# Own PSUM tiles for the first products of the experts, and a new table of priorities

## The chip, the cores and the metric

The kernel runs on one core of a Trainium2 chip. The metric is the device time of one execution in microseconds; for before it is the median of three runs. Engines are named as in the profile: PE is TensorE (matrix products), PEld its loading of weights, DVE VectorE, ACT ScalarE, POOL GpSimd, SP SyncE. A tile in PSUM holds results of products until another engine reads them; the widest accumulation here is [128, 512] fp32.

## The reference

Attention with 4 sink positions and a window of 128, then a layer of 8 experts of which each row takes two:

```python
# q, k, v: (4, 8, 768, 64)
scores = scale * np.matmul(q, k.transpose(0, 1, 3, 2))
keep = is_sink | in_window            # pos < 4, or 0 <= rel < 128
a = softmax(np.where(keep, scores, -1e9))
x = (a @ v).transpose(0, 2, 1, 3).reshape(3072, 512)

noisy = x @ w_gate + np.log1p(np.exp(x @ w_noise)) * noise   # 3072 x 8
top2, top2_w = the two largest of a row, softmax over the two
for e in range(8):                    # w1[e]: 512 x 1024, w2[e]: 1024 x 512
    for k in range(2):
        mask = top2[:, k] == e
        h = np.maximum(x[mask] @ w1[e], 0.0)
        out[mask] += top2_w[mask, k, None] * (h @ w2[e])
```

## The kernel before

**Two plans.** Every operation is given to a list scheduler (`Plan`) with an engine, an estimated length, a priority (a due time; the lowest goes first) and the keys that it reads and writes. `Plan.run` plays the operations through in model time, engine by engine, and then issues them in the order that comes out. So each engine's order is fixed in the program, and only semaphores between engines decide the times on the chip. `phase_one` holds attention, the logits, the routing of batches 0 to 2 and the first four row tiles of expert 0 (`FIRST`, gathered for the rows that batches 1 and 2 gave it, the fourth tile from batch 2 alone). `phase_two` holds the routing of batch 3 at priority -200 and then all experts, whose due times are worked out from 0 on (`when`, `step`).

The priorities of the attention stage come from the table `PR`: one number for each kind of step (score products `qk`, sink copies `pcopy`, transposes `ptr_c`, ...), with `_0` and `_9` for the first and last of a batch. Others set places: `gap` and `gap_8`, how many steps of attention lie between two pieces of a routing; `et`, from which step on the first row tiles come; `pc_pool`, how many of eight sink copies go to GpSimd; `stay`, how dear it is for TensorE to change the kind of product.

**An expert.** The rows of an expert are cut into pieces of three or four row tiles (for expert 0 four and then three, for the others three and then four). A piece q has eight groups f. For each group, TensorE makes twelve first products (`up`, L1048 to L1050: high part of the weights by high part of the rows, high by low, low by high, over four blocks of 128) into a PSUM tile H; ScalarE takes relu of it (`up_h`, L1097, the high part of h); VectorE takes what relu's rounding left (`up_l`, L1105, the low part of h, which reads H too). Then TensorE makes the second products of the group (`down`, L1116 to L1118, for the last tile L1121 and L1122) into four PSUM tiles Y that all groups of the piece add to. First products of the next group are due between them. In the last piece (`apart`) the first products of all eight groups come before its second products.

**PSUM.** A score tile S is [128, 2, 512] fp32, two accumulations wide, in a ring of two; it comes from a pool `wide` that lives through both phases. In phase two two more tiles of tag S are taken, and `plan.views` hands out their halves: H(k) is half k mod 2 of the one (`room`), X(i) half i mod 2 of the other (`pair`), which the routing and the row turns use. The first products of the first two groups (`AHEAD`) are issued by `up_ahead` at the end of phase one, into the same halves; from the third group on they are operations of phase two.

**Row tiles of expert 0.** `first_rows` gathers 128 rows by indirect DMA (L891), scales them on VectorE (L942), turns them on TensorE (`rows_turn`, L952; the fourth tile into a tile of tag S, the others into X), and splits them into a high part on ScalarE (L966) and a low part on VectorE (in the rows `sqn<-S,skn`, L215 being a helper that subtracts). They need the rank of a batch's rows (L714), the first product of its routing, and the places that come of it (L806). Logits are products L601 and transposes L609.

The loop that gives out the operations of the experts:

```python
if k >= AHEAD:
    op("PE", UP1 * width + .19, zu, lambda q=q, f=f: up(q, f), ..., w=[("H", k)], ...)
op("ACT", .06 + width / 1200, zu, lambda q=q, f=f: up_h(q, f), r=[("H", k)], w=[("hh", k)], u=[("h", k)])
op("DVE", .08 + width / 950, zu, lambda q=q, f=f: up_l(q, f), r=[("H", k), ("hh", k)], w=[("hl", k)], u=[("h", k)])
```

Of the kernel before, what the change touches and what calls it, by code (L numbers as in the profile page):

```python
# [9 lines left out]
F32 = mybir.dt.float32  # L10
# [10 lines left out]
PR = dict(cur=-8431.651, cur1=-7439.283, cur1_0=218.223, cur1_9=-1416.941, cur_0=0.0, cur_9=-191.213, dv=-2620.133,  # L21
          dv_0=-188.761, dv_9=-58.0, exps=-79.031, exps_0=-733.766, exps_9=-686.771, ga=0.0, gt=185.39, lg=-1781.795,
          load_qk=4173.715, load_v=245.644, mins=-994.502, mins_0=35.968, mins_9=5432.878, nosink=-4343.446,
          nosink_0=462.054, nosink_9=43.061, pcopy=-1854.216, pcopy_0=972.034, pcopy_9=77.513, plow=-3587.377,
          plow_0=-204.859, plow_9=-701.943, prev=-1305.7, prev_0=-151.842, prev_9=314.934, ptr=-349.555,
          ptr_0=-1749.435, ptr_9=-10.037, ptr_c=-3954.256, ptr_c_0=-264.44, ptr_c_9=56.179, ptr_m=-1635.596,
          ptr_m_0=182.224, ptr_m_9=-0.973, pv=-632.746, pv_0=479.582, pv_9=-76.04, pv_c=-4613.603, pv_c_0=-4.393,
          pv_c_9=16.777, qk=-1178.393, qk_0=631.58, qk_9=-3710.152, rows_c=12808.825, rows_c_0=-665.082,
          rows_c_9=-7472.954, rt=-15225.06, sink_c=-3756.417, sink_c_0=0.0, sink_c_9=16.368, sinks=-2.103,
          sinks_0=1336.99, sinks_9=-790.624, sub=-299.026, sub_0=1233.464, sub_9=50.854, sums=0.0, sums_0=723.554,  # L30
          sums_9=-13.305, sums_i=-3243.012, sums_i_0=-939.503, sums_i_9=-291.364, w1=4288.053, pctr_0=777.383,
          pctr=0.0, pctr_9=57.978, ga_l=-998.334, gt_l=111.981, ll=0.0, ua=22395.225, dv_pool=1, sm_act=10, cm_pool=9,
          pc_pool=0, gap_8=2, et=42, gap=1, stay=2496.59)
# [6 lines left out]
FIRST = 4  # L40
AHEAD = 2
# [7 lines left out]
class Plan:  # L49
# [5 lines left out]
    def __init__(self, nc, pools, rings, cold=0.0):  # L55
        self.nc = nc
        self.pools = pools
        self.rings = dict(rings)
        self.cold = cold
        self.live = {}  # L60
        self.views = {}
        self.shapes = {}
        self.count = {}
        self.ops = []
        self.touch = {}
        self.wrote = {}

    def get(self, tag, i, shape=None, dt=F32, pool="sb", pad=None):
        kx = (tag, i)
        if tag in self.views:  # L70
            x = self.views[tag](i)
            if shape is None:
                shape = self.shapes[kx]
            else:
                self.shapes[kx] = shape = (shape, pad)
            shape, pad = shape
            to = pad or shape
            x = x[:, :math.prod(to[1:])]
            if len(to) == 3:
                x = x.rearrange("p (a b) -> p a b", a=to[1])  # L80
            return x if to == shape else x[tuple(slice(0, n) for n in shape)]
# [163 lines left out]
def attention(tc, plan, cst, sh, kqs, v, vss, xbuf):  # L245
# [17 lines left out]

    def warm():
# [44 lines left out]
    def qk(n, a):  # L309
        g, j, _ = at(n, 2 * a)  # L310
        for h in range(2):
            r = slice(h * D, (h + 1) * D)
            p = get("S", 2 * n + a, [128, 2, 512], F32, "wide")[:, h, :2 * KW].rearrange("p (a b) -> p a b", a=2)
# [614 lines left out]
def rows_turn(plan, nc, cst, sh, e, t, size, ring, z):  # L928
# [15 lines left out]
    def spot():  # L944
        if ring == "S":
            return get(ring, ti, [128, 2, 512], F32, "wide")[:, 0, :].rearrange("p (c s) -> p c s", c=c)
        return get(ring, ti, [128, c, 128], F32, "ps")
# [91 lines left out]
def room(sh):  # L1039

    return sh.B * (sh.H // 2) * (sh.S // 128) + 1


# [20 lines left out]


def experts(tc, plan, cst, sh, w1, w2, xbuf, out):
# [97 lines left out]
    for q, (e, tiles, width) in enumerate(info):  # L1164
# [130 lines left out]
def phase_one(tc, nc, plan, ac, tail, cst, sh, kq, v, vs, w1, w2, xbuf, out):  # L1295
# [18 lines left out]
    def first_rows(t, ring, zg, zt):  # L1314
        gather(plan, nc, cst, sh, xbuf, 0, t, zg)
        weight(plan, nc, cst, sh, 0, t, zt)
        if ring == "S":
            plan.count["S"] = 2 * NJ * HP * sh.B - 1
# [136 lines left out]
```

## Time and profile before

| what | before |
|---|---|
| median of three runs | 787.09 us (786.73 to 788.6) |
| the profiled execution | 783.96 us |
| its span | 782.3 us, granted clock 0.998 |
| TensorE busy | 744.1 us, 95%, 4499 products |
| weight loads (beside the products) | 618.9 us, 79% |
| VectorE busy | 454.7 us, 58% |
| ScalarE busy | 333.4 us, 43% |
| GpSimd busy | 437.6 us, 56% |

The span is what the profiler saw of the engines' work in one execution; the time of that execution has a little more around it. Products overlap in the pipeline, so the duration of one in a timeline (0.34 us) is longer than the distance from its start to the next one's (0.17 us), and busy time counts the overlap once. In a timeline the bracket at the end of a row gives the engine's idle time just before it, and what ended that. The list of waits adds these up by the waiting line and the line that it waited for. Attention ends, and the experts begin, at about 186 us.

### The profile page before, as it was taken

What the parts mean: (1) busy time and instruction counts of PE and PEld (TensorE: products, weight loads), DVE (VectorE), ACT (ScalarE), POOL (GpSimd) and SP (SyncE); (2) the same over time, 40 slices, a digit from 0 to 9 for tenths busy, and PEclk for the clock granted to TensorE, in tenths of its full rate; (3) what the DMA queues carried; (4) which work ended last, traced back from release to release, by engine and by line L of the source; (5) the groups of instructions that cost most, each with busy time, mean ns of one, the idle gap of its engine ahead of it and who ended that gap; (6) DMA issues with size and microseconds to landing.
All of it is one profiled execution on the core that took longest, in us unless ns stands there. A gap on an engine that the chain in (4) does not pass through costs nothing.

```text
span 782.3 us, 12963 instructions
## 1 busy us (share of the span) xinstructions
PE 744.1 (95%) x4499; PEld 618.9 (79%) x4499; DVE 454.7 (58%) x1181; ACT 333.4 (43%) x927; POOL 437.6 (56%) x625
## 2 busy tenths in 40 slices
PE   9999998789999999999999999999999999999975
PEld 4667676566778898889888987898898889888864
DVE  7889998987754554645364446526544643464210
ACT  6987996784114413341333143323413431451211
POOL 7665878875246375356727462747275473747202
PEclk9999999999999999999999999999999999999999
DMA  6568698565636753553445363517452652544213
GB/s 221 175 169 203 203 261 216 138 162 132 168 96 127 238 110 50 156 138 57 94 127 131 53 134 114 109 40 155 123 101 47 172 134 36 125 133 71 26 16 41
DMA packets 58372, 97.80 MB, mean 125 GB/s; under 512 B 19232, under 2 KB 31776, under 8 KB 58304
## 3 DMA queue, kind: packets, MB, share of 16 engines
q1 hardware_dynamic: 44928, 69.34, 30.5%
q0 software_dynamic: 13376, 27.60, 20.3%
q8 instruction: 36, 0.59, 0.3%
q14 instruction: 32, 0.26, 0.1%
HBM read 68.51 MB, written 28.40 MB: 124 GB/s over the span
## 4 chain that ended last, share of the span: by engine, by line
PE 70%; DVE 9%; issue 7%; ACT 6%; POOL 3%; DMA 3%; POOLq 0%; SPq 0%; DVEq 0%; ACTq 0%
PE S L1048 11%; PE S L1050 10%; PE S L1049 10%; PE Y L1118 9%; PE Y L1116 9%; PE Y L1117 9%; PE S L315 2%; DMA xg<-x_rows,rt_idq 2%; PE X L406 2%; ACT cbuf L346 2%; PE P L380 1%; DVE h L1105 1%; PE X L409 1%; DVE xg L942 1%; POOL out L1140 1%
## 5 line engine op out<-in xcount | busy, mean ns | idle before, releaser
L897 POOL DMA_INDIRECT xg<-x_rows,rt_idq x174 | 176.1, 1012 | 62.2 <-issue 53.3
L1105 DVE SCALAR_TENSOR_TENSOR h<-S,h 128x384 fp32r<-128x384 f32 (+4 forms) x168 | 75.7, 470 | 203.5 <-ACT h L1097 153.2
L1097 ACT ACTIVATE h<-S 128x384 fp32r<-128x384 f32 (+4 forms) x128 | 64.3, 503 | 290.8 <-PE S L1050 210.1
L1048 PE MATMUL S<-skn,w 128*128 128x384 f32 (+4 forms) x512 | 177.7, 347 | 10.0 <-DVE h L1105 10.0
L1050 PE MATMUL S<-skn,w 128*128 128x384 f32 (+4 forms) x512 | 175.9, 344 | 0.0
L1049 PE MATMUL S<-sqn,w 128*128 128x384 f32 (+4 forms) x512 | 175.6, 343 | 0.0
L1140 POOL DMA_INDIRECT out<-y,idx x53 | 91.7, 1730 | 57.5 <-ACT y L1125 40.9
L1149 POOL COPY spacer<-h 1x1 f32<-1x1 f32 x88 | 28.7, 326 | 157.6 <-ACT h L1097 156.8
L1048 PEld LDWEIGHTS S<-skn,w 128*128 128x128 f32 x512 | 96.1, 188 | 22.4 <-DVE h L1105 10.4
L1049 PEld LDWEIGHTS S<-sqn,w 128*128 128x128 f32 x512 | 96.1, 188 | 6.2
L1050 PEld LDWEIGHTS S<-skn,w 128*128 128x128 f32 x512 | 96.0, 188 | 2.5
L1118 PE MATMUL Y<-w2a,h 128*128 128x512 f32 x192 | 76.1, 397 | 2.3 <-DVE h L1105 1.8
L1116 PE MATMUL Y<-w2a,h 128*128 128x512 f32 x192 | 75.7, 394 | 0.7 <-ACT h L1097 0.7
L1116 PE MATMUL Y<-w2b,h 128*128 128x512 f32 x192 | 76.1, 396 | 0.0
L1117 PE MATMUL Y<-w2b,h 128*128 128x512 f32 x192 | 75.8, 395 | 0.0
L1118 PE MATMUL Y<-w2b,h 128*128 128x512 f32 x192 | 75.8, 395 | 0.0
L1117 PE MATMUL Y<-w2a,h 128*128 128x512 f32 x192 | 75.6, 394 | 0.0
L315 PE MATMUL S<-kq 64*128 64x264 f32 (+1 forms) x384 | 56.4, 401 | 4.3 <-DVE cbuf L325 1.6
L215 POOL TENSOR_TENSOR cbuf<-cbuf,mn 128x528 f32<-128x528 f32 x48 | 51.4, 1076 | 13.4 <-DVE mn L335 5.5
L966 ACT ACTIVATE skn<-xtn 128x512 fp32r<-128x512 f32 (+2 forms) x46 | 27.9, 606 | 61.7 <-DVE xtn L957 54.7
L346 ACT ACTIVATE cbuf<-cbuf 128x132 f32<-128x132 f32 x160 | 48.0, 314 | 6.6 <-POOL cbuf L215 6.2
L1118 PEld LDWEIGHTS Y<-w2a,h 128*128 128x128 f32 x192 | 36.1, 188 | 14.0 <-DVE h L1105 4.8
(212 smaller groups left out, 1298.3 us busy)
## 6 DMA issues: line engine op xcount, KB each, us to landing
st<-in_w1l SPq DMA_DIRECT2D x32, 512.0 KB
st<-in_w2l SPq DMA_DIRECT2D x32, 512.0 KB
kq<-in_kq SPq DMA_DIRECT2D x15, 792.0 KB
out<-zt SPq DMA_DIRECT2D x31, 256.0 KB
vn<-in_v SPq DMA_DIRECT2D x16, 384.0 KB
x_rows<-xr SPq DMA_DIRECT2D x48, 128.0 KB
xg<-x_rows,rt_idq POOLq DMA_INDIRECT x174
st<-in_vs SPq DMA_DIRECT2D x4, 256.0 KB
```

The lines of the kernel that those rows point to most:

```text
L315: nc.tensor.matmul(p[:, :2 if j else 1], kq(g)[r, j // 2, 2 + j % 2, NS:], x[:, :2 if j else 1], start=True, stop=True)
L346: nc.scalar.activation(C(n)[:, u], C(n)[:, u], AF.Exp, scale=1.0 / math.sqrt(D), accum_out=get("sm", n, [128, 4])[:, u:u + 1])
L897: nc.gpsimd.indirect_dma_start(out=x[:, i, :], out_offset=None, in_=xbuf.rearrange("r (q d) -> (r q) d", d=sh.SW), in_offset=bass.Indirect ...
L1048: nc.tensor.matmul(p, w[:, 0], xh, start=(i == 0), stop=False)
L1049: nc.tensor.matmul(p, w[:, 0], xl, start=False, stop=False)
L1050: nc.tensor.matmul(p, w[:, 1], xh, start=False, stop=(i == sh.DM // 128 - 1))
L1097: nc.scalar.activation(get("h", FC * q + f, [128, 2 * 128 * FIRST], F32R)[:, :width], get("H", FC * q + f, [128, width], F32, "ps", [128, ...
L1105: nc.vector.scalar_tensor_tensor(h[:, o:o + s1 - s0], p[:, s0:s1], 0.0, h[:, s0:s1].bitcast(F32), op0=OP.max, op1=OP.subtract)
L1116: nc.tensor.matmul(p, hh, w[:, 0], start=(f == 0), stop=False)
L1117: nc.tensor.matmul(p, hh, w[:, 1], start=False, stop=False)
L1118: nc.tensor.matmul(p, hl, w[:, 0], start=False, stop=(f == FC - 1))
L1140: d = nc.gpsimd.indirect_dma_start(out=out, out_offset=bass.IndirectOffsetOnAxis(ap=c["idx"][:size(e, t), e, t:t + 1], axis=0), in_=get("y ...
```

## The change

**PSUM.** The pool `wide` and `plan.views` go. The score tiles S now belong to the PSUM pool of the attention phase (two of them are taken first, so that their place is set). Phase two has rings of its own in its own PSUM pool: two tiles H and two tiles X, each [128, 512] fp32. These take the place of tiles of phase one, and the pool of phase two makes the first user of such a tile wait for the last of the old one.

**No products at the end of phase one.** `up_ahead`, `AHEAD` and `room` go. The first products of the first two groups are operations of phase two like all others.

**Priority of expert 0's relu and low part.** For piece 0 these two steps get `zu - 400` instead of `zu`, ahead of the last routing's -200; the products keep `zu`.

**The table.** All numbers of `PR` are new, and `ua` is no longer used. Of the settings, `gap` goes from 1 to 2, `gap_8` from 2 to 3, `et` from 42 to 36, `pc_pool` from 0 to 2 and `stay` from 2496 to 1992.

```diff
-PR = dict(cur=-8431.651, cur1=-7439.283, cur1_0=218.223, cur1_9=-1416.941, cur_0=0.0, cur_9=-191.213, dv=-2620.133,
...
-          pc_pool=0, gap_8=2, et=42, gap=1, stay=2496.59)
+PR = dict(cur=-10653.273, cur1=-2090.412, cur1_0=-442.426, cur1_9=73.44, cur_0=-4.596, cur_9=0.0, dv=0.64,
...
+          gap_8=3, et=36, stay=1992.355)
-AHEAD = 2
...
-            p = get("S", 2 * n + a, [128, 2, 512], F32, "wide")[:, h, :2 * KW].rearrange("p (a b) -> p a b", a=2)
+            p = get("S", 2 * n + a, [128, 2, 512], F32, "ps")[:, h, :2 * KW].rearrange("p (a b) -> p a b", a=2)
...
-def up_ahead(plan, nc, cst, sh, f, z):
-
-    width = 128 * FIRST
-
-    def go(i):
-        up_block(plan, nc, sh, plan.get("S", room(sh), [128, 2, 512], F32, "wide")[:, f % 2, :width], 0, f, i, halves(plan, sh, 0), width)
-
-    for i in range(sh.DM // 128):
-        plan.op("PE", 3 * (width / 2400 + .016), z, lambda i=i: go(i),
-                r=[(x, 0, t) for x in ("xh", "xl") for t in range(FIRST)] + [w_tile(plan, 1, 0, f // 2)[0]], w=[("H", f)],
-                u=[("S", room(sh))])
...
-            if k >= AHEAD:
-                op("PE", UP1 * width + .19, zu, lambda q=q, f=f: up(q, f),
-                   r=[(x, e, t) for x in ("xh", "xl") for t in tiles] + [w_tile(plan, 1, e, f // 2)[0]], w=[("H", k)],
-                   u=[(nm, NP + q) for nm in ("skn", "sqn")])
-            op("ACT", .06 + width / 1200, zu, lambda q=q, f=f: up_h(q, f), r=[("H", k)], w=[("hh", k)], u=[("h", k)])
-            op("DVE", .08 + width / 950, zu, lambda q=q, f=f: up_l(q, f), r=[("H", k), ("hh", k)], w=[("hl", k)], u=[("h", k)])
+            op("PE", UP1 * width + .19, zu, lambda q=q, f=f: up(q, f),
+               r=[(x, e, t) for x in ("xh", "xl") for t in tiles] + [w_tile(plan, 1, e, f // 2)[0]], w=[("H", k)],
+               u=[(nm, NP + q) for nm in ("skn", "sqn")])
+            zh = zu if q else zu - 400
+            op("ACT", .06 + width / 1200, zh, lambda q=q, f=f: up_h(q, f), r=[("H", k)], w=[("hh", k)], u=[("h", k)])
+            op("DVE", .08 + width / 950, zh, lambda q=q, f=f: up_l(q, f), r=[("H", k), ("hh", k)], w=[("hl", k)], u=[("h", k)])
...
-    for f in range(AHEAD):
-        up_ahead(plan, nc, cst, sh, f, PR.get("ua", 60) + f)
...
-    plan.rings.update(y=4, h=9, X=2)
-    plan.count["X"] = 1
-    pair = plan.get("S", room(sh) + 1, [128, 2, 512], F32, "wide")
-    plan.views["X"] = lambda i: pair[:, i % 2]
-    plan.views["H"] = lambda i: plan.get("S", room(sh))[:, i % 2]
+    plan.rings.update(y=4, h=9, X=2, H=2)
+    for i in range(2):
+        plan.get("H", i, [128, 128 * FIRST], F32, "ps", [128, 512])
+    plan.get("X", 0, [128, NT + 1, sh.E], F32, "ps", [128, 64, 8])
```

What it moves on the engines, in three places. In the changed kernel line numbers are some 12 to 30 lower: L1048 to L1050 become L1031 to L1033, L1105 becomes L1075, L714 becomes L702.

**First pair: TensorE, from the last products of attention to the first products of expert 0.** L406, L409 and L418 (L394, L397 and L406 in the changed kernel) are products of attention, L601 and L609 (L589 and L597) those of the last logits, L940 is the row turn of the fourth tile. Before:

```order
L406 MATMUL X<-CT,vn 64x128 x4
L409 MATMUL X<-CM,dv 64x128 x4
L601 MATMUL X<-xtn,wbd 32x256 x4
L418 MATMUL X<-ps,vr 128x128 x2
L609 MATMUL X<-idf,lt 128x128 x2
L1048 MATMUL S<-skn,w_1580 128x512
L1049 MATMUL S<-sqn,w_1580 128x512
L1050 MATMUL S<-skn,w_1580 128x512
L601 MATMUL X<-xtn,wbd 32x256 x4
L609 MATMUL X<-idf,lt 128x128 x2
L1048 MATMUL S<-skn,w_1580 128x512
L1049 MATMUL S<-sqn,w_1580 128x512
```

and in the changed kernel:

```order
L394 MATMUL X<-CT,vn 64x128 x4
L397 MATMUL X<-CM,dv 64x128 x4
L406 MATMUL X<-ps,vr 128x128 x4
L589 MATMUL X<-xtn,wbd 32x256 x8
L940 MATMUL S<-idf,xg 128x128 x4
L597 MATMUL X<-idf,lt 128x128 x4
L1031 MATMUL H<-skn,w_1606 128x512
L1032 MATMUL H<-sqn,w_1606 128x512
L1033 MATMUL H<-skn,w_1606 128x512
```

The first products stood between the last logits and now stand behind all of them; the turn of the fourth row tile, which stood further ahead (L952), now stands ahead of the last four transposes L597.

**Second pair: TensorE, ahead of the rank of batch 2 (L714, now L702).** L315 (L303) are score products, L380 (L368) transposes of attention, L397 (L385) those of its sink columns. Before:

```order
L380 MATMUL P<-idf,cbuf 128x128 x4
L315 MATMUL S<-kq 128x132 x2
L315 MATMUL S<-kq 128x264 x2
L418 MATMUL X<-ps,vr 128x128 x6
L380 MATMUL P<-idf,cbuf 128x128 x4
L315 MATMUL S<-kq 128x264 x2
L397 MATMUL X<-idf,pcbuf 128x128
L714 LDWEIGHTS tri
L714 MATMUL X<-m,tri 128x48
```

and in the changed kernel:

```order
L397 MATMUL X<-CM,dv 64x128 x4
L394 MATMUL X<-CT,vn 64x128 x4
L397 MATMUL X<-CM,dv 64x128 x2
L406 MATMUL X<-ps,vr 128x128 x4
L368 MATMUL P<-idf,cbuf 128x128 x4
L303 MATMUL S<-kq 128x264 x2
L702 LDWEIGHTS tri
L702 MATMUL X<-m,tri 128x48
```

The two score products ahead of the rank in the changed kernel are the last of all; before, six more followed the rank. Of the rows between rank and first product of expert 0, the program of before has 8 transposes L380, 2 transposes L397, 12 products L406, 10 products L409, 6 products L418 and 12 row turns L952 more than the changed one, which has these ahead of the rank.

**Third pair: VectorE, tables of the last routing.** L789 to L796 (L777 to L784) make them, L828 (L816) uses them, and the subtraction on w2b is the low part of a chunk of weights. Before:

```order
L789 TENSOR_TENSOR y<-io,rt_pp 128x768
L793 TENSOR_TENSOR rt_tc_3498<-io_107,rt_tv 128x336
L793 TENSOR_TENSOR rt_tc_3500<-io_107,rt_tv 128x336
L796 TENSOR_TENSOR rt_tc_3498<-rt_tc_3498,tok 128x336
L796 TENSOR_TENSOR rt_tc_3500<-rt_tc_3500,tok 128x336
L215 TENSOR_TENSOR w2b<-st,w2b 128x1024
L1105 SCALAR_TENSOR_TENSOR h<-S,h 128x512
L828 SCALAR_TENSOR_TENSOR rt_idw<-S,ga 128x52
```

and in the changed kernel:

```order
L777 TENSOR_TENSOR y<-io,rt_pp 128x768
L1075 SCALAR_TENSOR_TENSOR h<-H,h 128x512
L781 TENSOR_TENSOR rt_tc_3502<-io_104,rt_tv 128x336
L781 TENSOR_TENSOR rt_tc_3504<-io_104,rt_tv 128x336
L784 TENSOR_TENSOR rt_tc_3502<-rt_tc_3502,tok 128x336
L784 TENSOR_TENSOR rt_tc_3504<-rt_tc_3504,tok 128x336
L200 TENSOR_TENSOR w2b<-st,w2b 128x1024
L816 SCALAR_TENSOR_TENSOR rt_idw<-X,ga 128x52
```

The first low part of expert 0 (L1105, now L1075) moved from behind the four table steps and the weights' low part to a place ahead of them.

## Rows read from the trace of the kernel before

**Rows 1.** List of waits, TensorE: from 186 us to the end, then from 735 us on.

```profile
PE S L1048 <- DVE h L1105: 10.0, 10, 1.6
PE Y L1118 <- DVE h L1105: 1.8, 6, 0.5
PE S L952 <- DVE gw L1031: 0.8, 1, 0.8
PE Y L1116 <- ACT h L1097: 0.7, 1, 0.7
PE Y L1118 <- DVE gw L1031: 0.5, 2, 0.3
...
PE S L1048 <- DVE h L1105: 5.4, 5, 1.2
```

**Rows 2.** Timeline, 744 to 748.4 us (start us, us, engine, line, operation [idle before]).

```profile
744.64 0.44 PE L1048 MATMUL S<-skn,w 128*128 128x384 f32 x1 [1.23 <-DVE h L1105]
...
745.28 0.34 PE L1048 MATMUL S<-skn,w 128*128 128x384 f32 x1
...
745.80 0.34 PE L1048 MATMUL S<-skn,w 128*128 128x384 f32 x1
...
747.11 0.49 ACT L1097 ACTIVATE h<-S 128x384 fp32r<-128x384 f32 x1 [3.11 <-PE S L1050]
...
747.63 0.56 DVE L1105 SCALAR_TENSOR_TENSOR h<-S,h 128x384 fp32r<-128x384 f32 x1 [3.04 <-ACT h L1097]
...
748.24 0.44 PE L1048 MATMUL S<-skn,w 128*128 128x384 f32 x1 [1.23 <-DVE h L1105]
```

**Rows 3.** Timeline, 261.9 to 262.7 us, VectorE and TensorE.

```profile
261.97 0.52 DVE L1105 SCALAR_TENSOR_TENSOR h<-S,h 128x256 fp32r<-128x256 f32 x2
...
262.63 0.39 PE L1048 MATMUL S<-skn,w 128*128 128x320 f32 x1 [1.35 <-DVE h L1105]
```

**Rows 4.** Windows, 0 to 186.5 us: length, busy PE, PEld, DVE, ACT, POOL, PEclk, DMA, GB/s.

```profile
0.00:186.50 186.50, 170.10 (x1669) 116.98 (x1669) 169.12 (x501) 148.21 (x635) 138.99 (x242) 1.00 0.68 187
```

**Rows 5.** Timelines of single engines, 161 to 185.6 us: batch 2's routing to expert 0.

```profile
161.10 0.20 PE L714 MATMUL X<-m,tri 128*128 128x48 bf16 x1
...
171.76 1.09 POOL L891 DMA_INDIRECT xg<-x_rows,idg  x1 [0.17 <-issue]
...
177.93 0.90 DVE L942 TENSOR_TENSOR xg<-xg 128x512 f32<-128x512 f32 x1
...
182.30 0.68 DVE L215 TENSOR_TENSOR sqn<-S,skn 128x512 fp32r<-128x512 f32 x1
...
185.07 0.48 PE L1048 MATMUL S<-skn,w 128*128 128x512 f32 x1
```

**Rows 6.** Chain that ended last, in order of time, 158 to 183 us (start us, us, what).

```profile
158.15 0.87 PE S L315 x8
...
180.02 0.44 PE S L952 x4
180.46 0.56 PE P L380 x4
181.02 0.59 PE X L406 x8
...
181.61 0.44 PE X L409 x8
182.04 0.57 PE X L601 x8
182.61 0.37 PE X L418 x2
```

**Rows 7.** Chain that ended last, 530 to 545 us: a gather.

```profile
539.16 4.38 DMA xg<-x_rows,rt_idq
```

**Rows 8.** Groups by line and shape, 0 to 190 us: GpSimd and ScalarE (busy us, mean ns of one).

```profile
L215 POOL TENSOR_TENSOR pcbuf<-cbuf,pcbuf 128x32 fp32r<-128x32 f32 x48 | 14.7, 307 | 13.8 <-ACT pcbuf L371 11.2 <-POOL cbuf L328 1.0 <-POOL cbuf L215 0.6
...
L371 ACT ACTIVATE pcbuf<-cbuf 128x32 fp32r<-128x32 f32 x48 | 11.1, 237 | 0.1
```

More of the change, by code (lines that the diff above doesn't have):

```diff
@@ L20 @@
 BIG = 1.0e30
-PR = dict(cur=-8431.651, cur1=-7439.283, cur1_0=218.223, cur1_9=-1416.941, cur_0=0.0, cur_9=-191.213, dv=-2620.133,
[L22 to L32, printed above, removed]
-          pc_pool=0, gap_8=2, et=42, gap=1, stay=2496.59)
@@ new lines @@
+PR = dict(cur=-10653.273, cur1=-2090.412, cur1_0=-442.426, cur1_9=73.44, cur_0=-4.596, cur_9=0.0, dv=0.64,
+          dv_0=-0.772, dv_9=-1.603, exps=3810.77, exps_0=-209.653, exps_9=-64.46, ga=2238.015, gt=27.108, lg=118.833,
+          load_qk=1899.239, load_v=208.527, mins=-1448.958, mins_0=0.0, mins_9=0.0, nosink=80.514, nosink_0=-636.435,
+          nosink_9=-1346.304, pcopy=-3801.108, pcopy_0=-245.281, pcopy_9=222.133, plow=84.759, plow_0=-186.727,
+          plow_9=0.17, prev=-3543.423, prev_0=4.494, prev_9=18.521, ptr=548.71, ptr_0=0.0, ptr_9=-0.149,
+          ptr_c=-4435.379, ptr_c_0=-197.723, ptr_c_9=-2504.924, ptr_m=-396.702, ptr_m_0=-645.517, ptr_m_9=119.683,
+          pv=-5.459, pv_0=0.0, pv_9=-34.884, pv_c=-7483.961, pv_c_0=190.698, pv_c_9=-316.386, qk=-1047.873,
+          qk_0=74.325, qk_9=0.0, rows_c=10040.612, rows_c_0=195.519, rows_c_9=-4.641, rt=-16496.065, sink_c=-5891.431,
+          sink_c_0=-111.387, sink_c_9=-669.979, sinks=-827.843, sinks_0=-159.469, sinks_9=-624.697, sub=270.819,
+          sub_0=-238.624, sub_9=-897.67, sums=0.0, sums_0=45.916, sums_9=-971.616, sums_i=-5384.046,
+          sums_i_0=-467.989, sums_i_9=-254.545, w1=8887.371, pctr_0=-29.914, pctr=800.069, pctr_9=-2964.751,
+          ga_l=-1277.079, gt_l=1521.637, ll=320.211, ua=-4.272, sm_act=10, dv_pool=1, cm_pool=9, pc_pool=2, gap=2,
+          gap_8=3, et=36, stay=1992.355)
@@ L60, in __init__ @@
         self.live = {}
-        self.views = {}
-        self.shapes = {}
         self.count = {}
@@ L69, in get @@
         kx = (tag, i)
[L70 to L81, printed above, removed]
         if kx not in self.live:
@@ L262, in vs @@
         return get("st", vst[b], [128, 1024], F32, "early").rearrange("p (a g h d) -> p a g h d", a=2, h=2, d=D)
+    for i in range(2):
+        get("S", i, [128, 2, 512], F32, "ps")
     def warm():
@@ L945, in spot @@
         if ring == "S":
-            return get(ring, ti, [128, 2, 512], F32, "wide")[:, 0, :].rearrange("p (c s) -> p c s", c=c)
+            return get(ring, ti, [128, 2, 512], F32, "ps")[:, 0, :].rearrange("p (c s) -> p c s", c=c)
         return get(ring, ti, [128, c, 128], F32, "ps")
@@ L1036, in weight @@
             w=[("wc", e, t)], u=[("wc", e), ("xg", n)])
-def room(sh):
-    return sh.B * (sh.H // 2) * (sh.S // 128) + 1
 def up_block(plan, nc, sh, p, e, f, i, both, width):
@@ L1317, in first_rows @@
         if ring == "S":
-            plan.count["S"] = 2 * NJ * HP * sh.B - 1
+            plan.count["S"] = 2 * NJ * HP * sh.B
         rows_turn(plan, nc, cst, sh, 0, t, 128, ring, zt)
@@ L1340, in phase_one @@
         w_chunk(plan, nc, cst, sh, w1, w2, 0, 2, i, PR.get("w1", 36) + 4 + i, "Pool", [("xt", 28 + 3 * i)])
-    for f in range(AHEAD):
-        up_ahead(plan, nc, cst, sh, f, PR.get("ua", 60) + f)
 def phase_two(tc, nc, plan, cst, sh, w1, w2, xbuf, out):
     b, NT = sh.B - 1, sh.S // 128
-    plan.rings.update(y=4, h=9, X=2)
-    plan.count["X"] = 1
-    pair = plan.get("S", room(sh) + 1, [128, 2, 512], F32, "wide")
-    plan.views["X"] = lambda i: pair[:, i % 2]
-    plan.views["H"] = lambda i: plan.get("S", room(sh))[:, i % 2]
+    plan.rings.update(y=4, h=9, X=2, H=2)
+    for i in range(2):
+        plan.get("H", i, [128, 128 * FIRST], F32, "ps", [128, 512])
+    plan.get("X", 0, [128, NT + 1, sh.E], F32, "ps", [128, 64, 8])
     plan.count["xtn"] = sh.B * sh.H // 2 - 1
@@ L1382, in moe_kernel @@
         experts_setup(nc, cst, sh, consts)
-        wide = both.enter_context(tc.tile_pool(name="wide", bufs=1, space=bass.MemoryType.PSUM))
-        pools = {"tail": tail, "early": early, "wide": wide}
+        pools = {"tail": tail, "early": early}
         with ExitStack() as st:
@@ L1394, in moe_kernel @@
             plan.run()
-            live = {kx: t for kx, t in plan.live.items() if kx[0] in ("st", "w1", "w2a", "xtn", "ri", "xg", "skn", "sqn", "lg", "S")}
+            live = {kx: t for kx, t in plan.live.items() if kx[0] in ("st", "w1", "w2a", "xtn", "ri", "xg", "skn", "sqn", "lg")}
         sb = both.enter_context(tc.tile_pool(name="msb", bufs=1, reuse_waits="tile"))
         ps = both.enter_context(tc.tile_pool(name="mps", bufs=1, space=bass.MemoryType.PSUM, reuse_waits="tile"))
-        p2 = Plan(nc, {"sb": sb, "ps": ps, **pools}, {kx: plan.rings[kx] for kx in ("st", "xtn", "ri", "xg", "lg", "S")})
+        p2 = Plan(nc, {"sb": sb, "ps": ps, **pools}, {kx: plan.rings[kx] for kx in ("st", "xtn", "ri", "xg", "lg")})
         p2.live.update(live)
```

## Prediction

> **What bounds the kernel now.** I read the page first: TensorE is busy for 95% of the span, and the last two thirds of it, the experts, are one nearly closed chain of products. So the time is TensorE's work plus TensorE's waits, and I looked for the waits next. The list of who waited for whom, from 186 us on, has five lines for TensorE [rows 1]: 20 waits, 13.8 us in all. The reader is to see that 19 of them, 13.0 us, are waits for the two halves of one step: ScalarE's relu (L1097) or VectorE's low part (L1105) of a first product, among them two where that low part itself stands behind VectorE's gate weights (L1031).
>
> Then I read the timeline around the longest of them, in the last piece, where the first products of all groups follow one another [rows 2]. There are two tiles' worth of space, so products of group f+2 should wait only for the readers of group f, and these have a whole group's time (12 products at 0.174 us, from 745.28 and 745.80, are 2.09 us) to do 0.49 + 0.56 us of work. Yet the group that starts at 744.64 and the next at 748.24 are 3.60 us apart. The relu at 747.11 starts when the group of 744.64 has ended, and the products of 748.24 when the low part after it has ended (747.63 + 0.56 us = 748.19). Whichever group that relu belongs to, the halves hold each other: if it reads the group just ended, the products of 748.24, which write the other half, need not have waited for it; if it reads the group before, whose products had ended before 744.64, it need not have waited until 747.11. Both halves are one tile (`room` tile of tag S), and the wait goes by tile. At 262.63 the same is seen from the other side [rows 3]: the products wait for the low part at 261.97, which reads the group just before, in the other half.
>
> **What each part costs or gives.**
>
> *Own tiles for H.* With a ring of two tiles a group waits for the group two before. In the last piece the products that start at 744.64 take 0.10 + 11 x 0.174 + 0.34 = 2.35 us, to 746.99, and their readers are done at 748.19, 1.2 us later, inside the 2.09 us of the next group; in the other pieces second products lie between as well. All 19 waits go. What each is worth: the step of 3.60 us less 2.09 us is 1.51 us, while the view records 1.23 us of idle [rows 2], since the end of the product before and the slow first product (0.44 us against 0.34) hide 0.28 us. So 13.0 + 19 x 0.28 = 18.3 us. The bounds: 13.0 us if the hidden part is only there in the last piece, and 13.8 + 20 x 0.28 = 19.4 us if the 0.8 us at L952 goes too. I take 18.3 us, because rows 2 show the hidden part directly.
>
> [...]
>
> *No products ahead of the last routing's plan.* `up_ahead` goes; the same 24 products are issued in phase two. No work is added or lost. But in before they start between the last logits; now they stand behind all of them (the first pair of order rows). After the first product before still has 1.0 us of logits to do (one group L601 of 0.57 us, and two pairs L609 at 0.22, half a group L952) [rows 6].
>
> *The table of numbers.* It moves nearly every instruction of the attention stage. The counts of instructions stay, but for 12 of the 48 copies of sink columns, which go from ScalarE (237 ns each) to GpSimd, where the nearest row is the subtraction on the same tile at 307 ns [rows 8]: 2.8 us off one engine, 2.8 to 3.7 us onto another, and neither bounds: GpSimd is busy for 139.0 of 186.5 us, ScalarE for 148.2, TensorE for 170.1 and VectorE for 169.1 [rows 4]. So the stage is held by TensorE and VectorE together, with 16.4 us of TensorE time unused. A new order could win at most these 16.4 us, or lose as much again; with equal work on both engines I take 0.
>
> One place of that order can be priced, and it costs. The fourth row tile of expert 0 needs batch 2's routing: rank (L714), place, gather, scaling, turn, high and low part, and then the first product. Before, rank, gather, scaling, low part and product stand at 161.10, 171.76, 177.93, 182.30 and 185.07 [rows 5]: with 0.68 us for the low part the chain takes 21.9 us, hidden below 24.0 us of other TensorE work. In the new order the rank stands behind the last score product (second pair of order rows). Counted in the order, 6 score products (L315), 8 transposes L380, 2 L397, 12 L406, 10 L409, 6 L418 and 12 row transposes L952 that followed the rank now precede it. The chain counts each L315, L406, L409 and L601 twice, the order once, so by the order one costs 0.22, 0.14, 0.11 (as for L952), 0.15, 0.11, 0.19 and 0.11 us [rows 6], and together they cost 8.0 us. The rank comes 8.0 us later, and of the 25.0 us (24.0 and the 1.0 above) 17.0 are left to cover the chain. The chain could be shorter than 21.9 us where it queued before: the gather lands 4.4 us after its start in the quickest row [rows 7] (a quarter of the size, so I take 5.5), then scaling, turn, high and low at 0.6 to 0.7 us each with 0.2 us between; that is 161.10 to 171.76 plus 5.5 plus 3.1, or 19.3 us. So the products of expert 0 begin 19.3 - 17.0 = 2.3 us to 21.9 - 17.0 = 4.9 us later. I take 3.6 us, the middle. What is queued behind: the turn of that tile (L940) now stands ahead of the last two logits transposes on TensorE, so the last routing waits with it. That wait is the 3.6 us already counted; the last routing feeds only the rows of the pieces behind, which TensorE reaches after the first piece.
>
> *Expert 0's low parts first.* On VectorE one low part moves ahead of the routing's tables and w2b's low part (third pair of order rows). It delays the last routing by one such step, under 0.7 us, and TensorE does not wait for that routing at either point but the 0.8 us at L952. I count 0, with -0.8 to +0.7 us as bounds; the first is in the bound of 19.4 us above.
>
> **Sum.** -18.3 + 3.6 + 0 = -14.7 us. The profiled execution of before took 783.96 us (span 782.3), 3.1 us under the median of the three runs, 787.09; the sum is a difference and goes to both: 769.3 us for an execution like the profiled one, 772.4 us as the median. I predict **772.5 us**.
>
> **The rivals.**
>
> 1. *The waits stay* (slower). If the low part and the relu were late for a reason of their own (a ring of two being too short, or the two engines' hand-over), own tiles change nothing and only the later start is left: 787.1 + 3.6 = 790.7 us. For it: the waits name VectorE. Against it: readers need 1.2 us and have 2.09. It decides if the step of the last piece stays above 3 us. Chance 0.03. [...]
> 2. *The seam takes more.* The gather also waits for the writes of batch 2's weights, and the new attention order may leave TensorE or VectorE idle longer than before. Another 4 to 10 us there gives 776.5 to 782.5 us. For it: rank and last score product are now neighbours, and VectorE is nearly as full as TensorE. Against it: the total work is the same. Chance 0.20. To end no faster it would have to cost 14.7 us more, nearly doubling the unused TensorE time of the stage; chance 0.04, at about 787 us.
> 3. *The waits come back behind the products.* The low part then holds the second products instead, where VectorE is late. At 262.63 the products had stood still for 1.35 us, from 261.28 [rows 3]. With own tiles the twelve of 320 columns would run from there, 12 x 0.174 x 320/384 = 1.74 us, until 263.02, and the low part that the second products need ends at 261.97 + 0.52 = 262.49: 0.5 us of margin. The last piece has five of the ten waits at L1048, with 5.4 of the 10.0 us [rows 1], and no second products between. If the other five come back in full, 4.6 + 5 x 0.28 = 6.0 us are lost: 778.4 us. Chance 0.08.
> 4. *The new order is also the better one.* If it wins back 5 us or more of the 16.4 us unused in attention: 767 us and below. Nothing in the rows speaks for it but that there is room. Chance 0.13.
>
> **How the numbers follow.** The forecast, 768 to 777 us, has 0.52. Below it lies rival 4 (0.13), above it rivals 2 and 3 (0.28 together), then the two that end at or above before (0.07). The range of 8 in 10 leaves out the lower end of rival 4 and what lies at or above before: 764 to 782 us. A difference of 0.3% (2.4 us) is about what a measurement of this kernel can tell from none. Faster: all but rivals 1 and the extreme of 2, 0.93. Within 0.3%: 0.03, from that extreme. Slower: 0.04.
>
> **What would show it.** Right: in the last piece starts of groups 2.1 us apart, and TensorE's waits for h below 2 us in total from the first product of the experts on; the relu starts 0.3 us after its own group. The first product of expert 0 at 186 to 192 us, with TensorE idle for several us ahead of it, behind the turn L940. Wrong: any group of first products that waits for the low part of the group directly before it; or a first product later than 196 us.

## The result, and the profile after

| | before | after |
|---|---|---|
| median of four runs | 787.38 us (786.73 to 788.6) | 774.02 us (773.63 to 774.65) |
| ratio, 95% interval | | 0.983 (0.981 to 0.985) |
| the profiled execution, its span | 783.96, 782.3 us | 774.65, 773.0 us |
| TensorE busy | 744.1 us, 95% | 741.7 us, 96% |

The changed kernel is 13.4 us faster; 14.7 us were forecast. The page of the changed kernel, busy times and one of the costliest groups (out<-in, count | busy us, mean ns | idle just before):

```profile
PE 741.7 (96%) x4499; PEld 623.8 (81%) x4499; DVE 458.7 (59%) x1181; ACT 334.3 (43%) x915; POOL 439.8 (57%) x637
...
L1031 PE MATMUL H<-skn,w 128*128 128x384 f32 (+4 forms) x512 | 176.1, 344 | 0.1
```

L1031, the first of the first products, had 10.0 us of idle time before it (as L1048, [rows 1]) and now has 0.1. The list of TensorE's waits from 180 us on, without the shortest:

```profile
PE X L385 <- POOL pcbuf L200: 4.3, 1, 4.3
PE X L597 <- ACT lt L593: 1.3, 2, 0.7
PE X L394 <- ACT ps L401: 0.5, 1, 0.5
PE X L940 <- issue: 0.3, 1, 0.3
PE H L1032 <- DVE sqn L200: 0.3, 1, 0.3
```

No product waits for relu or low part any more; the 19 waits of [rows 1] are gone, and the last two lines are all the waiting that is left from the first product on. The timeline of the last piece shows what replaced the steps of 3.60 us of [rows 2]:

```profile
737.72 0.33 PE L1031 MATMUL H<-skn,w 128*128 128x384 f32 x1
...
737.98 0.49 ACT L1067 ACTIVATE h<-H 128x384 fp32r<-128x384 f32 x1 [1.42 <-PE H L1033]
...
738.50 0.56 DVE L1075 SCALAR_TENSOR_TENSOR h<-H,h 128x384 fp32r<-128x384 f32 x1 [2.93 <-ACT h L1067]
...
739.82 0.34 PE L1031 MATMUL H<-skn,w 128*128 128x384 f32 x1
741.91 0.34 PE L1031 MATMUL H<-skn,w 128*128 128x384 f32 x1
```

Groups start 2.10 and 2.09 us apart, as forecast, and the relu starts 0.3 us behind the start of the next group, while that group runs. From the first product to the end of the span it was 597.2 us, of which 1.0 us were logits (782.3 - 185.07, [rows 5]); now it is 577.1 us (773.0 - 195.90). The experts won 19.1 us.

The seam lost. These rows, from single engines' timelines, are the way to the first product of expert 0 (162.37 is there for comparison):

```profile
162.37 0.66 PE L394 MATMUL X<-CT,vn 128*64 128x128 f32 x8
...
170.08 0.20 PE L702 MATMUL X<-m,tri 128*128 128x48 bf16 x1
...
185.17 1.09 POOL L879 DMA_INDIRECT xg<-x_rows,idg  x1 [5.67 <-DMA out<-zt]
186.26 0.27 POOL L200 TENSOR_TENSOR pcbuf<-cbuf,pcbuf 128x32 fp32r<-128x32 f32 x1
...
186.59 0.48 PE L385 MATMUL X<-idf,pcbuf 128*128 128x128 f32 x1 [4.33 <-POOL pcbuf L200]
187.00 1.12 PE L394 MATMUL X<-CT,vn 128*64 128x128 f32 x8
...
195.90 0.47 PE L1031 MATMUL H<-skn,w 128*128 128x512 f32 x1
```

The rank comes 9.0 us later than in [rows 5], about as worked out (8.0). The gather then starts 13.4 us later (185.17 against 171.76), and the first product 10.8 us. The gather's own row says what happened: GpSimd stood at it for 5.67 us. Behind it on GpSimd stands the low part of the last sink columns (186.26), and TensorE waited 4.33 us for that. When TensorE went on, the product L394, which takes 0.66 us for eight at 162.37, took 1.12. The windows of the changed kernel (us, busy PE, PEld, DVE, ACT, POOL, granted clock, DMA share, GB/s) show the clock that TensorE had there:

```profile
182.00:187.00 5.00, 0.67 (x5) 0.20 (x3) 2.95 (x9) 0.00 (x0) 1.82 (x3) 0.91 0.14 21
187.00:191.00 4.00, 3.45 (x31) 3.05 (x32) 2.36 (x4) 0.45 (x2) 4.00 (x6) 0.50 0.51 166
191.00:196.50 5.50, 4.65 (x37) 3.10 (x34) 3.01 (x8) 2.98 (x6) 0.24 (x2) 0.82 0.84 203
```

Over the 5 us with 0.67 us of work the granted clock was 0.91 in the mean, for the next 4 us it was 0.50, and over the 5.5 us behind them 0.82. What sets it, these rows do not show. What stands ahead of the gather is to be seen on SyncE's queue:

```profile
169.87 6.94 SPq L425 DMA_DIRECT2D x_rows<-xr  x12
176.90 2.28 SPq L728 DMA_DIRECT2D x_rows<-rt_w  x4
```

Twelve writes of batch 2's attention rows, 6.94 us of issuing, stand just ahead of the four writes of its routing weights. The gather reads rows and weights. Its index (L820) and its own waits for semaphores in the same execution:

```profile
179.77 0.14 DVE L820 SCALAR_TENSOR_TENSOR idg<-X,ga 128x1 int32<-128x1 f32 x1
...
L879 POOLq EVENT_SEMAPHORE  x4: 43/43/43, 184.1 to 184.4; - x4
```

The index was ready at 179.91 us. By the times of landing in the trace, the last row write had landed at 179.21 us, the last of the weights' writes at 184.09, and the first of the gather's waits ended at 184.11. So the last thing that the gather waited for were the weights' writes, which were issued and landed behind the rows. The write of zeros that the bracket names landed at 184.64 us, when these waits were over.

### The profile page after: what moved, and what is told of

The parts are those of the page before. It is cut to its first block, busy times and chain, and to the rows that moved or that the text cites. A ratio compares the mean times of both kernels' runs of the same rounds, so it can differ in the third digit from the quotient of the medians.

```text
span 773.0 us, 12926 instructions
## 1 busy us (share of the span) xinstructions
PE 741.7 (96%) x4499; PEld 623.8 (81%) x4499; DVE 458.7 (59%) x1181; ACT 334.3 (43%) x915; POOL 439.8 (57%) x637
## 4 chain that ended last, share of the span: by engine, by line
PE 66%; issue 4%; POOL 2%; DMA 2%; SPq 0%; ACT 0%; DVE 0%; POOLq 0%; ACTq 0%
PE H L1031 11%; PE H L1033 11%; PE H L1032 11%; PE Y L1086 10%; PE Y L1087 10%; PE Y L1088 10%; POOL out L1110 1%; PE Y L1091 1%; PE Y L1092 1%; DMA out<-y,idx 1%; DMA st<-in_w1l 1%; SPq L1261 0%; PE X L940 0%; POOL xg L885 0%; DVE w L200 0%
## 5 line engine op out<-in xcount | busy, mean ns | idle before, releaser
L1067 ACT ACTIVATE h<-H 128x384 fp32r<-128x384 f32 (+4 forms) x128 | 64.6, 504 | 265.9 <-PE H L1033 230.1
L1075 DVE SCALAR_TENSOR_TENSOR h<-H,h 128x384 fp32r<-128x384 f32 (+4 forms) x168 | 75.8, 471 | 172.5 <-ACT h L1067 153.2
L1031 PE MATMUL H<-skn,w 128*128 128x384 f32 (+4 forms) x512 | 176.1, 344 | 0.1
L1032 PE MATMUL H<-sqn,w 128*128 128x384 f32 (+4 forms) x512 | 175.7, 343 | 0.3 <-DVE sqn L200 0.3
L1033 PE MATMUL H<-skn,w 128*128 128x384 f32 (+4 forms) x512 | 175.9, 344 | 0.0
L1032 PEld LDWEIGHTS H<-sqn,w 128*128 128x128 f32 x512 | 96.1, 188 | 7.5 <-DVE sqn L200 0.7
L1031 PEld LDWEIGHTS H<-skn,w 128*128 128x128 f32 x512 | 96.1, 188 | 7.5 <-PE X L597 0.3
L1033 PEld LDWEIGHTS H<-skn,w 128*128 128x128 f32 x512 | 96.0, 188 | 2.5
L200 POOL TENSOR_TENSOR cbuf<-cbuf,mn 128x528 f32<-128x528 f32 x48 | 53.0, 1104 | 22.3 <-DVE mn L323 9.6
L303 PE MATMUL S<-kq 64*128 64x264 f32 (+1 forms) x384 | 57.5, 406 | 4.6 <-DVE cbuf L313 4.0
L303 PEld LDWEIGHTS S<-kq 64*128 64x128 f32 x384 | 30.4, 188 | 21.0 <-DVE cbuf L313 9.9
```

The costliest lines, as they stand in the source:

```text
L200: eng.tensor_tensor(out, a, b, op=OP.subtract)
L303: nc.tensor.matmul(p[:, :2 if j else 1], kq(g)[r, j // 2, 2 + j % 2, NS:], x[:, :2 if j else 1], start=True, stop=True)
L1031: nc.tensor.matmul(p, w[:, 0], xh, start=(i == 0), stop=False)
L1032: nc.tensor.matmul(p, w[:, 0], xl, start=False, stop=False)
L1033: nc.tensor.matmul(p, w[:, 1], xh, start=False, stop=(i == sh.DM // 128 - 1))
L1067: nc.scalar.activation(get("h", FC * q + f, [128, 2 * 128 * FIRST], F32R)[:, :width], get("H", FC * q + f, [128, width], F32, "ps", [128, ...
```

## The experiments

Each time is a median of five or more runs, with its ratio to before on the same chip (786.0 to 786.5 us there) and the 95% interval. The changed kernel was not run again beside them: its 774.02 us goes with a before of 787.38 us. Differences to 774.02 us are therefore uncertain by some 2 us; e11, which moves a single write of zeros, ran at 773.52 to 778.08 us.

| kernel | time, us | ratio to before |
|---|---|---|
| e1: changed, halves again | 796.04 | 1.014 (1.011 to 1.016) |
| e2: before, own tiles alone | 766.04 | 0.974 (0.972 to 0.977) |
| e3: changed, weights' writes first | 776.28 | 0.989 (0.986 to 0.991) |
| e4: changed, old table | 768.03 | 0.978 (0.975 to 0.980) |
| e5: changed, rows first | 770.47 | 0.980 (0.977 to 0.983) |
| e6: changed, gather behind | 775.45 | 0.986 (0.983 to 0.989) |
| e7: e5 and e6 | 770.11 | 0.980 (0.977 to 0.983) |
| e8: e2, low parts first | 768.9 | 0.980 (0.976 to 0.983) |
| e9: e4, low parts at their due time | 780.86 | 0.993 (0.991 to 0.995) |
| e10: changed, low parts at their due time | 782.46 | 0.996 (0.994 to 0.998) |
| e11: changed, zeros behind | 776.34 | 0.988 (0.986 to 0.990) |

**e1, halves again.**

```diff
-    plan.rings.update(y=4, h=9, X=2, H=2)
-    for i in range(2):
-        plan.get("H", i, [128, 128 * FIRST], F32, "ps", [128, 512])
+    plan.rings.update(y=4, h=9, X=2, H=2, HH=1)
+    both = plan.get("HH", 0, [128, 2, 512], F32, "ps")
+    plan.halves = lambda k: both[:, k % 2]
```

> The changed kernel, but the first products write the two halves of one tile again; no instruction changes its place on any engine. Theory (a wait goes by tile, so halves hold each other, and that is the whole gain in the experts): the waits of TensorE for relu and low part come back, 16 to 20 us, so 790 to 794 us against 774.0. Rival (the gain comes from the new order and the earlier low parts; the tiles do not matter): 773 to 776 us.

796.04 us, 22.0 more than the changed kernel, a little above the range. The list of waits from 199 us on, and the first product:

```profile
PE HH L1031 <- DVE h L1075: 10.8, 10, 1.9
PE Y L1088 <- DVE h L1075: 1.7, 5, 0.6
PE Y L1086 <- ACT h L1067: 0.7, 1, 0.7
PE Y L1088 <- DVE gw L1019: 0.5, 2, 0.3
...
198.07 0.47 PE L1031 MATMUL HH<-skn,w 128*128 128x512 f32 x1 [0.29 <-DVE sqn L200]
```

The same four lines as in [rows 1], 18 waits with 13.7 us, in the order of the changed kernel. So it is the shared tile and not the order that makes the waits. From the first product to the end of the span it was 595.9 us (794.0 - 198.07), 18.8 us more than in the changed kernel; the rest of the 22.0 us lies ahead of that, where the first product came 2.2 us later with the same order, and in the 2 us of uncertainty. The wait follows the tile that the program declares: from the first product on TensorE waits 13.7 us for relu, low part and gate weights with one tile of two halves, and for none of them with the two tiles of the changed kernel.

**e2, own tiles alone.** In the kernel before, group k writes half 0 of tile k mod 2 (those of `up_ahead` too), and the routing and row turns take half 1:

```diff
+    duo = [plan.get("S", room(sh)), pair]
-    plan.views["X"] = lambda i: pair[:, i % 2]
-    plan.views["H"] = lambda i: plan.get("S", room(sh))[:, i % 2]
+    plan.views["X"] = lambda i: duo[i % 2][:, 1]
+    plan.views["H"] = lambda i: duo[i % 2][:, 0]
```

> The kernel before, but first products k go to half 0 of tile k mod 2 and the other X results to half 1, so that two groups in a row share no tile; every engine's order is that of before. Theory: 18.3 us fewer than before and nothing at the seam, 787.4 - 18.3 = 769.1 us, 768 to 771, which is faster than the changed kernel. Rival (tiles do not matter): 787 us. If the other X results, now beside H, hold the products, some 1 to 2 us of it are lost in the first two pieces.

766.04 us: 20.4 us under before with no instruction moved, 2 us below the range, and 8.0 us under the changed kernel. Its first product:

```profile
190.70 0.48 PE L1048 MATMUL S<-skn,w 128*128 128x512 f32 x1
```

From there to the end of the span it was 578.2 us (768.9 - 190.70), against 597.2 us in before: 19.0 us less. From 184 us on TensorE's waits are 0.9 us in all. This is the fastest version measured here.

**e4, the old table.** All of the change but `PR`, which is that of before:

> The changed kernel with the table of numbers of before: own tiles, no products ahead of the last logits, low parts of expert 0 first, but attention in the order of before, the weights' writes ahead of the row writes again. Theory (the new table costs the time at the seam): 787.4 - 18.3 + 1.0 = 770.1 us, 769 to 772, and the first product at about 186 us. Rival (the missing products ahead, not the table, cost it): 774 us or more.

768.03 us, 1 us below the range. The new table costs 774.02 - 768.03 = 6.0 us by the medians; by the spans of the two profiled executions it is 8.2 us (773.0 and 764.8), by the ratios to before some 4 us (0.983 and 0.978). So its cost is known to be between 4 and 8 us. Timelines of SyncE, GpSimd and TensorE with the old table:

```profile
148.11 4.25 SPq L425 DMA_DIRECT2D x_rows<-xr  x8
...
155.41 3.71 SPq L425 DMA_DIRECT2D x_rows<-xr  x4
...
163.00 2.99 SPq L728 DMA_DIRECT2D x_rows<-rt_w  x4
...
171.76 1.09 POOL L879 DMA_INDIRECT xg<-x_rows,idg  x1 [0.17 <-issue]
...
187.30 0.48 PE L1031 MATMUL H<-skn,w 128*128 128x512 f32 x1
```

Here batch 2's rows are written from 148.11 to 159.1 us, ahead of the routing's weights; the gather starts at 171.76, as before, and the first product at 187.30.

**e3, weights' writes first.** My first reading of SyncE's rows was that the weights come too late, since the row writes stand ahead of them:

```diff
-    plan.dma(z if last else plan.now, keep, 1.2, r=[t("w")], w=[("wrow", gid)], n=4)
+    plan.dma(z if last else plan.now - 1000, keep, 1.2, r=[t("w")], w=[("wrow", gid)], n=4)
```

> The changed kernel, but SyncE issues the four writes of batch 2's weights ahead of eight of the twelve row writes that stand before them; nothing else moves. Theory (the gather waits for these writes behind the row writes, GpSimd's sink columns wait behind the gather, and TensorE waits for them and then runs at half its clock): the writes start some 5 us earlier, so does the gather, TensorE's wait of 4.3 us ahead of the last sink columns goes and the first product comes 5 to 8 us earlier: 766 to 769 us. Rival (the later rank alone sets the first product): 773 to 775 us.

776.28 us, above both ranges: nothing was gained. The writes of the weights moved, and the gather did not come earlier:

```profile
172.83 2.32 SPq L728 DMA_DIRECT2D x_rows<-rt_w  x4
175.25 6.13 SPq L425 DMA_DIRECT2D x_rows<-xr  x8
...
186.12 1.08 POOL L879 DMA_INDIRECT xg<-x_rows,idg  x1 [6.29 <-DMA out<-zt]
```

The weights were issued by 175.15, 11 us ahead of the gather's start, and had landed by 181.05 us. But now the rows stood last: the last of their writes landed at 185.04 us, and the gather's waits ended from 185.06 us on. The gather waits for the last of the sixteen writes, whichever that is, and the edit only exchanged rows and weights.

**e5, rows first.** VectorE's turns of batch 2's rows (L420) and their writes are issued soon after their inputs, all else in its place:

```diff
+        for i, d in self.ahead.items():
+            start[i] = min(start[i], d + (max(start[j] for j in self.ops[i][4]) if self.ops[i][0] == "SP" else at[i]))
...
+            if b == 2:
+                plan.ahead[len(plan.ops) - 1] = 2.0
```

> The changed kernel, but VectorE's turns of batch 2's attention rows, and the twelve writes of these rows on SyncE, are issued soon after their inputs are there and not in one block behind; every other instruction keeps its place. Theory (the gather for expert 0's fourth row tile reads these rows, so it waits for their writes; all else at the seam follows from that): the gather starts at 180 to 181 us instead of 185.2, TensorE no longer waits for the last sink columns and keeps its clock, the first product comes at 189 to 190 instead of 195.9: 767 to 769 us. Rival (the rank's place and the weights' writes behind it set the gather): above 772 us.

```profile
145.59 6.34 SPq L430 DMA_DIRECT2D x_rows<-xr  x8
...
171.99 2.21 SPq L737 DMA_DIRECT2D x_rows<-rt_w  x4
...
181.66 1.08 POOL L888 DMA_INDIRECT xg<-x_rows,idg  x1 [0.89 <-DVE ids L870]
...
191.26 0.47 PE L1040 MATMUL H<-skn,w 128*128 128x512 f32 x1
```

The gather started 3.5 us earlier, GpSimd stood at it for 0.89 us, for an index of VectorE's and no longer for a write, TensorE's wait of 4.3 us is gone, and the first product came 4.6 us earlier. The weights, issued 4.9 us earlier without the rows ahead of them, had landed by 179.43 us. The time is 770.47 us, 3.5 us less than the changed kernel; 5 to 7 were expected. By the spans of the profiled executions it is 4.2 us (773.0 and 768.8), and e7 against e6 below, which differ by this edit alone and ran on one chip, 5.3 us. So the late rows, with the weights behind them, are what held the gather, and they are half or more of what the table costs.

**e11, zeros behind.** The profile names a write of zeros as what ended the gather's wait. It was moved behind the next load of weights:

> The changed kernel, but the write of zeros that SyncE issues right behind batch 2's rows and weights (the one named as what ended the gather's wait) stands behind the next load of weights. Theory (the gather waits for rows and weights; the zeros only end in the same stretch): the gather starts at 184.5 to 185.5 us and the time is 773 to 775 us. Rival (the gather waits for the zeros too): it starts 1 us or more earlier, and the time is 770 to 773 us.

```profile
185.16 1.09 POOL L882 DMA_INDIRECT xg<-x_rows,idg  x1 [5.37 <-issue]
```

The gather started at the same time, as the theory had it, and the time, 776.34 us, is no better (1.3 us above the theory's range). The name in the bracket is only that of a write which ended in the same stretch.

**e6, gather behind.** The gather stands behind the low part of the sink columns on GpSimd, which is all that moves:

```diff
+        for i, j in self.behind.items():
+            start[i] = max(start[i], start[j] + .001)
...
+        if t == FIRST - 1:
+            plan.behind[len(plan.ops) - 1] = plan.last
```

> The changed kernel, but on GpSimd that gather stands behind the low part of the last sink columns instead of ahead of it; nothing else moves. Theory (TensorE's wait of 4.3 us and the low clock after it come from that low part standing behind the waiting gather): the gather still starts at 185.2 us, but TensorE does the rest of attention meanwhile; the first product comes at 191 to 193 us: 770 to 772 us. Rival (TensorE's wait is not what delays the first product, the gather alone is): 773 to 775 us.

775.45 us, 0.4 us above the rival's range: no gain. TensorE did the rest of attention at once, and then stood at the row turn:

```profile
186.94 1.08 POOL L885 DMA_INDIRECT xg<-x_rows,idg  x1 [6.02 <-DMA out<-zt]
...
192.09 1.11 PE L948 MATMUL S<-idf,xg 128*128 128x128 f32 x4 [4.89 <-DVE xg L938]
...
194.89 0.77 PE L1039 MATMUL H<-skn,w 128*128 128x512 f32 x1
```

It waited 4.89 us there instead of 4.33 us earlier, and the turn and the first products fell into the low clock (0.50 from 191 to 196.5 us). One premise of both theories did not hold: the gather started at 186.94 instead of 185.17 us, since the last of the weights' writes landed at 185.86 us in this execution. From the gather's start to the first product it took 8.0 us, against 10.7 in the changed kernel, so the edit did shorten that way; later writes, and more of the low clock behind the first product (one at 196.73 us still took 0.63 us, against 0.39 to 0.40 in the changed kernel from its second on), took it back. What the edit is worth with the writes at their old time is not shown.

**e7, both.**

> Both edits together. If the late rows are the root, the second edit adds nothing to the first: 767 to 769 us, within 0.7 us of the kernel with rows first. If the two are separate causes, it is 2 us or more below either.

770.11 us, 0.4 us from e5, as expected of one root, though 1.1 us above the range. With the rows early, the second edit adds nothing that can be measured.

**e10 and e9, low parts at their due time.**

```diff
-            zh = zu if q else zu - 400
+            zh = zu
```

> The changed kernel without the earlier priority of expert 0's relu and low parts. Theory (worth nothing): 773.3 to 774.7 us. Rival (without it TensorE waits for low parts behind the routing's tables): 775 us or more, with a wait of second products for L1075 in the first piece.

782.46 us, 8.4 us more than the changed kernel. That is in the rival's range, but the wait that the rival named is not there. Of the waits of TensorE from 180 us on:

```profile
PE X L385 <- POOL pcbuf L200: 6.4, 1, 6.4
PE X L841 <- DVE rt_idr L830: 2.5, 1, 2.5
PE X L940 <- DMA xg<-x_rows,idg: 1.5, 1, 1.5
...
PE X L940 <- PE H L1033: 0.4, 1, 0.4
```

> The kernel with own tiles and the old table (768.0 us), without the earlier priority of expert 0's relu and low parts. Theory (that priority is worth nothing, and the missing products ahead make the 2 us to the kernel of before with own tiles, 766.0): 767.3 to 768.7 us. Rival (the earlier low parts cost 1 to 2 us, since they delay the last routing): 766 to 767 us.

780.86 us, 12.8 us more than e4. Its waits, and the window from 200 to 225 us (us, busy PE, PEld, DVE, ACT, POOL, clock, DMA share, GB/s):

```profile
PE X L940 <- DVE xg L930: 6.6, 1, 6.6
PE X L841 <- DVE rt_idr L830: 1.9, 1, 1.9
PE X L940 <- DVE sqn L200: 1.2, 1, 1.2
```

```profile
200.00:225.00 25.00, 15.14 (x74) 11.79 (x73) 15.45 (x43) 3.90 (x7) 6.88 (x10) 0.73 0.60 167
```

These are not waits for low parts. L841 is a product of the last routing and L940 the row turn of expert 0's second piece. Without the priority the plan has VectorE do the routing first, takes its results to be ready earlier, and so puts these products further ahead on TensorE: the first L841 stands 113 products behind the first product of expert 0 in e9 and e10, against 140 in e4 and 164 in the changed kernel. On the chip VectorE is not done by then, and all first and second products stand behind them: 9.7 us in e9, with a clock of 0.73 in that window. From the first product to the end of the span e9 has 590.0 us (779.5 - 189.49), e4 577.5 (764.8 - 187.30): 12.5 us, nearly all of the difference. In e10 these waits are 4.4 us, and from its first product at 197.81 us to the end it is 582.0 us, 4.9 us more than in the changed kernel. The rest of the 8.4 us is not the priority's as far as is shown: the wait at the seam (L385) is 2.1 us longer in e10, but every instruction that the edit moves comes behind 199 us, and e1 with the order of the changed kernel waits 5.0 us there.

**e8, low parts first with the old order.**

> The kernel before with first products in different tiles (766.0 us in the run of that edit alone), and relu and low part of expert 0's first piece ahead of the last routing as in the changed kernel. Theory (that priority is worth nothing, since TensorE waits neither for the routing nor for these low parts there): 765 to 767 us. Rival (earlier low parts free the H tiles earlier and gain): 764 us or less; or it delays the last routing's rows, and TensorE waits for them at the second piece: 768 us or more.

768.9 us, above the theory's range, with an interval that meets that of e2. TensorE waits 1.0 us at a row turn that shares its tile with an H in this arrangement. Whether the rest of the 2.9 us to e2 is real is open.

## Why the prediction was right, and where it was off

**Own tiles: right, and the largest term.** Forecast 18.3 us, from steps of 3.60 us that should become 2.09. Steps became 2.10, the experts' stretch 19.1 us shorter; undoing this part alone cost 22.0 us, 18.8 of them in that stretch (e1), doing it alone gave 20.4, with 19.0 in that stretch (e2). The hidden 0.28 us for each wait belonged in the sum: the waits as recorded, 13.0 us, would have been too little.

**The table: mis-sized.** The prediction had 0 for the order as a whole and 3.6 us for the place at the seam. The table cost 6.0 us by the medians, and 4 to 8 us by all that was measured (e4). The step that failed is the chain from rank to first product: it followed the routing's steps and let the gather start when its index is there. But the gather also waits for sixteen writes to the rows that it reads. The turns of batch 2's attention rows on VectorE and their twelve writes on SyncE had moved as well, to 169.87 us, and the weights' four writes stood behind them; the last of these landed 4.2 us after the index was ready (184.09 and 179.91). That is worth 3.5 to 5.3 us (e5; e7 against e6). What is left with the rows early, 2.4 us by the medians (770.47 - 768.03), fits the later rank, for which the prediction's bounds were 2.3 to 4.9 us; no run moves the rank alone. Its second rival had the right place and the right writes (the gather waits for the weights of batch 2, 4 us or more); what it did not have is that the row writes stand ahead of these.

**What would show it.** Forecast was a first product at 186 to 192 us behind a wait at the turn L940; it came at 195.90, and the wait stood further ahead, at L385, behind the gather on GpSimd's queue. The prediction asked what is queued behind the turn, and not what is queued behind the gather.

**Products ahead.** 1.0 us was forecast for their loss. e4, which lacks them, is 2.0 us above e2, which has them, but low parts and tiles differ too, so this stays unsettled.

**Low parts first: 0 was the wrong question.** The prediction looked at what one step more on VectorE delays. The priority's effect is on TensorE: it keeps the routing's products from being placed too early. Against before the term is small, because that plan had them late enough (the first product of that step, L853 there, stands 173 products behind the first product of expert 0, and TensorE waits 0.8 us at L952, [rows 1]); within the new plan it is worth 4.9 us in the experts (e10), and 12.5 us there with the old table (e9).

**The sum.** By the profiled executions the experts won 19.1 us and the seam lost 9.8 (10.8 less the 1.0 us of logits), in all 9.3 (782.3 to 773.0), against 14.7 forecast. By the medians it is 13.4. The difference is in before: its profiled execution, at a mean clock of 0.998, was 3.4 us under the median of its runs, and that of the changed kernel 0.6 us above its own. Carrying the difference over to the median unchanged helped the forecast by some 4 us that it had not worked out. To that extent the agreement of 772.5 with 774.02 us is luck: by the profiled executions the seam lost 6.2 us more than the 3.6 forecast, which is what the second rival describes.

## What to carry to other kernels

Where a reader waits for work that it does not read, look at which tile the two share: here the waits were 13.7 us with two halves declared as one tile (e1) and gone with two tiles (the changed kernel), and splitting a tile can be tried without moving an instruction (e2, 20.4 us). The gather waited here for the last of the sixteen writes to the rows that it may read (landed at 184.09 us, waits ended from 184.11 in the changed kernel; 185.04 and 185.06 in e3), and for its index where that came last (0.89 us in e5). So the chain to it is to be followed from the later of the two, and moving one of the writes ahead of another gained nothing (e3, 776.28 us). After a change of priorities, look at each engine for instructions that the plan takes to be ready and the chip does not: the engine stood at them with all that was queued behind (TensorE 6.6 us at L940 in e9, GpSimd 5.67 us at the gather in the changed kernel).

## What the runs showed of the hardware

Behind the same wait the granted clock of TensorE was 0.50 in one execution and 1.00 in another. The wait of TensorE and a window of 2 us behind it in the profiled execution of e2, whose order is that of before:

```profile
PE P L380 <- ACT cbuf L346: 0.9, 1, 0.9
...
178.00:180.00 2.00, 1.63 (x12) 1.23 (x8) 0.39 (x1) 1.44 (x5) 0.77 (x2) 0.50 0.01 5
```

and the same in before:

```profile
PE P L380 <- ACT cbuf L346: 0.9, 1, 0.9
...
178.00:180.00 2.00, 2.00 (x21) 1.65 (x22) 1.83 (x4) 2.00 (x8) 2.00 (x4) 1.00 0.01 4
```

With the same longest wait ahead of it (at 174.37 us in e2, at 171.06 in before), e2 ran at 0.50 from 178 to 182 us, and before at 1.00 in every window of 2 us from 170 to 182. This profiled execution of e2 took 770.45 us at a mean clock of 0.988; its other runs took 764.12 to 766.54 at 0.992 to 0.998. In the changed kernel, with its wait of 4.3 us, all four runs have a mean clock of 0.992 to 0.994 and lie within 1.0 us; in e11, with nearly the same order, six runs have 0.987 to 0.993 and lie within 4.6 us. So two executions of one program differed by more than 2 or 3 us, and a difference of that size between two profiled executions is to be read from medians.
